# A new order table for a five-engine attention and gated-mixer kernel

## The chip, the cores and the metric

One core of a Trainium2 chip. The time is device microseconds of one execution; of several executions the median is given. The profile is of one execution, taken by the hardware profiler; its span runs from the first to the last instruction.

## What is computed

The reference runs a gated linear recurrence over 768 steps for 4 batches and 8 heads of width 48, and feeds its output, as rows of 384, to a spatially gated mixer:

```python
for t in range(S):
    state = alpha[:, :, t, :, None] * state + einsum('bhd,bhe->bhde', k[:, :, t], v[:, :, t])
    y[:, :, t] = einsum('bhd,bhde->bhe', q[:, :, t], state)
x = y.transpose(0, 2, 1, 3).reshape(B, S, H * D)           # 4, 768, 384
h = maximum(x @ w_in, 0)                                    # 1024 columns
u, v = h[..., :512], h[..., 512:]
v_n = (v - mean(v)) / sqrt(var(v) + 1e-6)                   # over the 512 columns
v_s = einsum('ts,bsd->btd', w_spatial, v_n) + b_spatial[None, :, None]
out = (u * v_s) @ w_out
```

Inputs and output are float32; the matmuls of the kernel take bfloat16.

## The kernel before

**Tiling.** The recurrence is cut into chunks of 128 steps, 6 for each batch, 24 in all, numbered i. The first 8 chunks are done two at a time as pairs 0 to 3 (function `pair`), the rest singly (`first`). For a chunk or pair: ScalarE takes the logarithm of alpha (`lnp`, L446, or `ln`, L654); TensorE sums it along the steps with a triangle of ones (`cump`, L455, or `cum`, L660 and L663); ScalarE takes two exponentials of that (L463 and L472, or L672 and L689); the keys are multiplied by one (`ktp`, L477, or `kt`, L684), the queries by the other (`qtp`, L484, or `qt`); the values are cast (`vbp`, `vb`). TensorE transposes keys and queries (L505, or `trk` L713 for a single chunk); the results are evicted (`ev`). TensorE forms the scores (`sc`, L577 or L748), VectorE masks them (`m`, L588 or L759), TensorE multiplies them by the values (`ya` L604, `y` L617, or `y` L770 and L776). The state's update is a matmul (`updq` L539 and L547, or `upd` L734); `z` adds it (L331, L333), `S` scales it on GpSimd (L338), `sb` casts it. ScalarE casts y (`xs`), TensorE transposes it (`xt`, L368 or L392), `xe` evicts it.

The mixer runs for each batch b: `v`, one group of 3 matmuls a chunk (L822), relu by ScalarE, statistics `bn` (L887, L888), `rs` (L911, L912) and normalization `vn` (L919); `u`, 8 groups of 3 matmuls with relu; `s`, 8 groups of 6 matmuls with w_spatial, emitted in two halves of 3, with the bias added by VectorE (L968) and the gate product `g` (L981) after it; `o`, 6 groups of 4 matmuls, evicted and stored. The last `o` of all is done in two half-width parts (`oh`). w_spatial is transposed on TensorE once (`wt`, L834) and evicted (`we`).

**Kinds of TensorE blocks.** `sc`, `trk`, `wt`, `ya`, `updq` and the `xt` of single chunks use matmuls whose operands hold 48 or 64 rows; the others use all 128 rows.

**What sets the order.** Every operation is an entry of a list; PLAN, a table in the source, names them by number in the order in which they are emitted, with a letter for the engine: P TensorE, D VectorE, A ScalarE, G GpSimd, S a DMA issue on SyncE's queue, Q a DMA as such (which emits nothing). Each engine runs its own operations in the table's order; waits between engines are put in from the data that they share. A P entry can carry numbers, `P43:512:512:192`: matmuls on a tile of constants, so many columns each, put ahead of the block (L188). `replay` (L112) walks the table; `bank` (L176) gives out the 8 PSUM banks in turn. One operation can hold instructions of two engines: operation 3, `("cz", 2)`, is listed under G, and its function `zeros(2)` emits one VectorE memset of `mask4` and three GpSimd instructions (L274, L275, and L279, which fills `mask4` after the memset):

```python
            if n == 2:
                nc.vector.memset(mask4.bitcast(FP32), 0.0)
                nc.gpsimd.memset(ut_ones, 0.0)
                nc.gpsimd.affine_select(
                    out=ut_ones, in_=ut_ones, compare_op=ALU.is_gt, fill=1.0,
                    base=0, channel_multiplier=1, pattern=[[-1, 128]],
                )
                nc.gpsimd.affine_select(
                    out=mask4, in_=mask4, compare_op=ALU.is_gt, fill=1.0,
                    base=0, channel_multiplier=1, pattern=[[0, 4], [-1, 128]],
                )
```

**Loads.** A pair's alpha, keys, queries and values are loaded in 384 KB pieces (L435), those of single chunks in 192 KB pieces (L640) into halves of a tile that two chunks share; weights come in 768 KB pieces (L1072) through two buffers and are cast by any of three engines. Stores are issued at L1037, the two last half-width ones at L1011. All of these go through SyncE's one queue; the bias alone is issued by GpSimd.

Of the kernel before, what the change touches and what calls it, by code (L numbers as in the profile page):

```python
# [62 lines left out]
D176 P138 G185 P83 A139 D175 A80 P140 A84 D186 P178 A143 P180 D179 A177 G187 P188 P190 Q308 S309 D189 G129 P144 P192
D181 A145 D191 A141 G6 D194 A193 A8 P197 D7 Q10 P200 G195 D199 P85 S14 A315 G196 D198 P157 A86 G130 D201 P316 A158
P146 D202 Q312 A317 D159 A318 P203 A147 P204 P208 D87 P88 A205 Q310 A209 G11 P206 D12 P326 A89 D13 P210 A207 D320
P151 S18 Q15 A211 D148 S313 P212 A327 S367 G319 A328 P324 D152 P223 A213 D330 G329 P215 A160 D90 A325 Q19 P334 S371
P322 A216 P221 D162 G16 A224 D217 P153 A222 P332 G17 A91 D323 P229 A335 P225 D92 Q314 S22 D231 A154 P149 D93 A333
G20 D214 P232 A226 P227 A150 Q368 D230 S369 P155 D234 A228 D161 A233 P235 D21 Q372 A218 S409 D237 P238 A236 D219
P344 G321 A156 Q23 D239 P255 S446 D220 G331 P259 D345 A375 P376 D346 P336 A377 A378 A380 P260 D338 Q370 S373 A240
D381 P256 A337 D261 A24 P263 G339 Q410 D257 S411 P264 D25 G379 P241 Q447 D341 P347 A242 S448 D265 P251 A243 G342  # L70
D349 Q374 P244 P383 G340 S413 A245 D246 P252 D348 A417 G262 P275 Q412 A385 S415 D253 P276 D384 G258 A382 Q449 P350
D277 A454 S450 P390 A351 G343 P267 D391 Q414 P418 S480 G278 D392 P354 P352 A419 P279 Q416 A353 S26 G421 P268 A355
P386 A420 A422 P356 D269 Q451 G266 P393 S482 A357 D387 P280 A394 D423 G388 P455 Q481 D281 S484 P395 A457 P425 A456
G389 P361 D427 A424 Q27 D397 G458 A396 S452 P358 D426 A459 A362 D460 P398 G254 A359 D363 P428 A399 P462 G270 P432
D429 A488 P271 D433 A463 G430 Q483 S577 P401 D464 P489 D434 A28 G31 P407 Q485 A490 G30 S486 D400 P272 A492 P435 A402
G491 Q453 D29 P405 S581 A436 D273 P283 G282 A408 D493 Q578 S579 P437 P469 A284 G274 D438 P495 A406 D470 P403 Q487
A496 S611 G461 D471 P287 A439 G431 A497 Q582 D404 P291 S583 A288 D360 P465 P498 Q580 A585 S648 P472 D466 A292 D500
P586 G494 A364 P440 Q612 G467 D499 A587 S690 P295 A473 G468 D366 A588 A590 Q584 S615 P474 A441 G589 P501 D475 D591
P299 Q649 A502 D442 S728 A476 P503 A296 P593 G592 P477 A619 Q691 D505 D504 S613 A300 D594 P517 D365 A478 Q616 P596
D595 S650 P506 A443 D597 A479 D518 P513 Q729 D445 S652 A507 P600 D444 P620 A508 D602 Q614 P519 S692 A621 P533 D509  # L80
A656 P303 Q651 S694 A514 D601 P515 A510 Q653 A622 P525 A698 D512 S617 D511 A624 P529 G623 D516 A520 Q693 P657 S654
P534 A304 D625 G598 A659 A658 P526 D535 Q695 G599 A661 S732 P699 D527 P530 A701 A700 G660 P545 Q618 A703 D531 S730
A736 P627 G536 P603 D629 Q655 P546 S762 A604 D704 G528 P537 A628 D662 Q733 P538 S696 D547 G626 P605 P664 D539 G702
A606 P634 Q731 A607 P630 S766 A665 P541 D631 G663 A666 D635 P737 Q763 G632 P542 S858 A738 D636 G548 A739 P671 A741
P706 Q697 D543 S892 P667 A708 G532 P608 D742 A707 D672 Q767 P521 S764 G740 A609 P637 D633 A770 P549 Q859 A638 S734
D668 P522 D673 P550 Q893 G705 D523 S862 P639 P744 D551 A640 P713 G524 A641 Q765 D746 P674 A745 S860 D714 P771 G669
A675 P642 D715 A772 Q735 G670 S768 A774 P751 P676 A643 P553 G540 D678 Q863 D677 A866 S864 D775 P709 P716 A554 G773
D752 P679 Q861 A717 S929 D753 A900 G544 P557 A680 D710 Q769 D610 S896 P777 G711 A558 P718 P867 A743 G712 Q865 P561
D719 A869 D779 S933 A868 D720 A681 P747 G552 D778 P686 Q930 D644 S894 P721 A871 G870 A562 P754 D748 Q897 A722 D872
S971 P565 G749 A755 D687 G750 A645 Q934 P780 P874 S931 A566 D782 P756 P569 G776 A757 A723 Q895 D781 G873 S975 P573  # L90
D876 A758 A875 P783 D724 Q972 S898 P682 A784 A570 P881 D646 Q932 P785 P759 S973 D787 A786 D883 A574 P788 A937 Q976
D882 S935 A760 P796 D683 A789 P684 Q899 D761 S1012 A797 P877 P800 A685 D790 Q974 A725 P901 S1008 P688 A903 A801 D647
P794 A979 Q936 D726 S1042 P938 A791 D727 P798 D878 A902 Q1013 D792 P810 A940 A905 S1046 D793 G904 P802 A939 D795
P980 Q1009 D906 G879 S1010 P803 A981 P811 G941 A799 D804 Q1043 A942 P806 S977 D689 A982 G805 A984 P807 D812 Q1047
P884 S571 D943 P822 G907 A885 D985 P823 G813 Q1011 D808 S1044 P908 P886 G983 P945 A910 D887 Q978 P814 D909 S1014
A888 D824 P911 A946 G809 P815 D912 Q572 A947 P889 S1048 D816 G944 A1016 Q1045 S575 D880 P987 A890 G817 P915 P952
A988 D916 Q1015 P1017 G913 P830 A1050 D989 A1019 G914 P834 A1018 D917 Q1049 A1021 P1051 D953 G825 P838 A1052 Q576
D954 A835 P948 G1020 P831 A1054 D949 P918 D832 G950 P818 A919 D1022 G986 P819 A839 D1055 G951 P920 P1024 D820 A921
P994 A1025 G1053 D922 P990 P826 D996 A1026 P955 G1023 D995 P827 G833 A956 D991 P1031 D828 P957 P1057 G992 A959 D1032
P923 A958 G821 A1059 D1033 P960 A924 G829 P997 A1058 D925 P967 A998 G993 P1027 A961 P999 P1060 D1028 A968 P842 D962  # L100
G1029 A1000 A1001 P963 G1030 A843 D1061 P1002 A1056 S844 D1062 A964 P1034 S305 A1003 D891 P850 S836 Q845 A1035 S840
P1063 D1004 Q306 P846 A1064 Q837 A926 P1065 P1036 A847 P965 D1067 Q841 D1037 A1038 D1066 P854 D928 D966 P1068 A851
D927 A1005 P969 A1069 D1006 P1074 D1007 P1039 D1070 P1078 A1040 P1080 A855 D1041 P1076 A970 S856 P1090 S297 D1075
A1071 P1094 S285 D1079 A1077 Q857 P1082 S289 D1072 P1106 Q298 D1073 S301 D1081 P1086 Q286 S567 P1087 Q290 S563 P1083
D1088 Q302 S852 P1095 G1089 Q568 P1091 S559 D1096 P1102 Q564 S293 D1092 G1097 P1098 D1084 Q853 S848 P1103 D1093 Q560
G1085 S555 P1099 D1104 Q294 P1107 D1105 P1113 Q849 D1100 Q556 P1117 A1114 D1108 G1101 P1110 D1109 S1115 A1118 P1111
S1119 P1121 D1112 Q1116 P1137 A1122 Q1120 P1125 D1138 S1123 P1133 S1139 A1126 P1129 D1134 Q1124 S1127 S1135 A1130
# [1040 lines left out]
```

## Time and profile before

| | us |
|---|---|
| median of 3 runs | 146.05 (145.07 to 146.84) |
| span of the profiled execution | 142.9 |
| last matmul's end in it | 139.55 |
| last store's landing in it | 141.98 |

The profiled execution's own time outside the span is not recorded; its span is 3.1 us below the median of the runs. In section 1 of the page each engine has its busy time, its share of the span and its instructions; section 2 cuts the span in 40 slices, each digit the busy share in tenths; section 4 is the chain of work that ended last. In lines of the timeline the first number is the start, the second the time to the end of the piece; the piece's own line, operation, output and inputs follow, and in brackets the idle time before it and what ended it. Matmuls are pipelined: a block's cost to TensorE is the distance from its start to the next block's start, not its duration.

### The profile page before, as it was taken

The page shows a single profiled execution, that of the slowest core. Times are in us where ns is not written, and L with a number is a line of the kernel's source. Part 1 is how long each engine was busy: PE and PEld are TensorE (multiplying, and loading weights), DVE is VectorE, ACT ScalarE, POOL GpSimd, SP SyncE. Part 2 cuts the span into 40 slices and gives each one's busy share as a digit, 9 for nine tenths or more (in the row PEclk, how much of TensorE's full clock was granted, in tenths as well). Part 3 has the DMA queues.
Part 4 walks back from the last instruction along what each step waited for, and adds up shares of the span by engine and source line. Part 5 has one row for each costly group of instructions (what it writes and reads, how often), then busy time and mean ns, then how long its engine had stood idle before and what let it go on. Part 6 is the DMA issues. An engine that isn't in the chain of part 4 may idle for free.

```text
span 142.9 us, 4962 instructions
## 1 busy us (share of the span) xinstructions
PE 132.9 (93%) x1910; PEld 83.7 (59%) x1923; DVE 122.2 (85%) x290; ACT 108.2 (76%) x280; POOL 86.0 (60%) x147
## 2 busy tenths in 40 slices
PE   7978977999799999999999999999999999999990
PEld 3464857456465666665655666656666666556460
DVE  6759998998989799989789999889889989776950
ACT  3567398899976799999987889999878688760131
POOL 6945853748317999971288879910999994003700
PEclk9999999999999999999999999999999999999999
DMA  4999989999998999999899999999999103229645
GB/s 115 268 261 265 250 201 327 334 322 328 251 224 163 213 276 161 203 176 198 145 205 192 164 209 162 208 143 206 187 156 222 55 7 137 86 98 338 229 150 180
DMA packets 89000, 28.64 MB, mean 200 GB/s; under 512 B 83728, under 2 KB 87440, under 8 KB 88976
## 3 DMA queue, kind: packets, MB, share of 16 engines
q1 hardware_dynamic: 88944, 28.32, 92.0%
q8 instruction: 15, 0.25, 0.8%
q14 instruction: 9, 0.07, 0.2%
q0 software_dynamic: 32, 0.00, 0.0%
HBM read 23.60 MB, written 4.72 MB: 198 GB/s over the span
## 4 chain that ended last, share of the span: by engine, by line
PE 70%; DMA 10%; SPq 6%; ACT 6%; DVE 3%; issue 2%; ACTq 0%
PE bank L822 50%; DMA ac<-in_alpha_dram 10%; SPq L435 6%; PE bank L748 3%; PE bank L713 3%; PE bank L776 2%; PE bank L660 2%; ACT v_sb L204 2%; PE bank L734 2%; PE bank L770 2%; PE bank L392 2%; DVE stats L887 1%; DVE vn L919 1%; ACT x_sb L198 1%; PE bank L663 1%
## 5 line engine op out<-in xcount | busy, mean ns | idle before, releaser
L822 PE MATMUL bank<-w_spT,vn 128*128 128x384 bf16 x192 | 36.3, 326 | 0.0
L981 POOL TENSOR_TENSOR gT<-vsb,uT 128x384 bf16<-128x384 f32 x28 | 25.8, 928 | 14.2 <-DVE vsb L968 13.5
L822 PEld LDWEIGHTS <-vn 128*128 128x128 bf16 x192 | 16.8, 97 | 10.5 <-DVE vn L919 0.2
L684 POOL TENSOR_TENSOR kt<-kc,binv 128x384 bf16<-128x384 f32 x16 | 14.8, 924 | 12.6 <-ACT bc L679 6.6
L759 DVE TENSOR_TENSOR ptm<-bank,mask 128x512 bf16<-128x512 f32 x32 | 20.8, 683 | 0.6 <-PE bank L748 0.6
L822 PE MATMUL bank<-xT,w_in 128*128 128x384 bf16 x96 | 19.7, 326 | 0.1
L968 DVE TENSOR_TENSOR vsb<-bank,bsp_bc 128x384 f32<-128x384 f32 x31 | 16.6, 552 | 3.0 <-PE bank L822 1.6
L822 PE MATMUL bank<-w_out_sb,gT 128*128 128x384 bf16 (+1 forms) x100 | 18.6, 319 | 0.0
L822 PE MATMUL bank<-w_in,xT 128*128 128x512 bf16 x59 | 16.9, 379 | 1.1 <-issue 0.3
L198 ACT COPY kqT<-bank 128x512 bf16<-128x512 bf16 x26 | 14.8, 592 | 1.3 <-PE bank L713 0.8
L338 POOL TENSOR_TENSOR state<-state,bc 128x192 f32<-128x192 f32 x20 | 10.4, 518 | 8.8 <-ACT bc L553 6.4
L887 DVE BATCH_NORM_STATS2 stats<-v_sb 128x6 f32<-128x512 bf16 x20 | 13.7, 683 | 1.4 <-ACT v_sb L204 1.4
L198 ACT CAST x_sb<-bank 128x384 bf16<-128x384 f32 x24 | 11.5, 485 | 2.2 <-PE bank L776 1.9
L204 ACT ACTIVATE v_sb<-bank 128x512 bf16<-128x512 f32 x20 | 11.6, 601 | 1.6 <-PE bank L822 1.5
L822 PEld LDWEIGHTS <-gT 128*128 128x128 bf16 x100 | 8.9, 97 | 5.6 <-POOL gT L981 0.4
L200 POOL CAST sbd<-state 64x192 bf16<-64x192 f32 x32 | 10.9, 341 | 1.7
L822 PEld LDWEIGHTS <-w_in 128*128 128x128 bf16 x96 | 8.3, 97 | 5.3 <-issue 0.4
L198 ACT COPY xT<-bank 128x192 bf16<-128x192 bf16 (+1 forms) x25 | 8.7, 384 | 2.9 <-PE bank L392 2.6
L919 DVE TENSOR_SCALAR vn<-v_sb,mvs,rstd 128x512 bf16<-128x512 bf16 x24 | 9.8, 437 | 0.7 <-ACT rstd L912 0.7
L588 DVE TENSOR_TENSOR ptm<-bank,mask 128x512 bf16<-128x512 f32 x16 | 10.3, 676 | 0.0
L188 PE MATMUL bank<-junk 128*128 128x512 f32 (+4 forms) x24 | 9.3, 490 | 1.1 <-DVE junk L234 1.1
L200 DVE COPY kqT<-bank 128x512 bf16<-128x512 bf16 x22 | 9.0, 417 | 1.5 <-PE bank L505 0.9
(131 smaller groups left out, 288.2 us busy)
## 6 DMA issues: line engine op xcount, KB each, us to landing
ac<-in_alpha_dram SPq DMA_DIRECT2D x16, 192.0 KB, 4.6
qc<-in_q_dram SPq DMA_DIRECT2D x16, 192.0 KB, 4.7
kc<-in_k_dram SPq DMA_DIRECT2D x16, 192.0 KB, 4.8
vc<-in_v_dram SPq DMA_DIRECT2D x16, 192.0 KB, 4.3
...
```

Of the source, the lines that this page charges most:

```text
L198: nc.scalar.copy(out=out, in_=in_)
L200: ENG[eng].tensor_copy(out=out, in_=in_)
L204: nc.scalar.activation(out=out, in_=in_, func=AF.Relu)
L338: ENG[eng].tensor_tensor(out=st["state"], in0=st["state"], in1=st["bc"][:, :, None].to_broadcast([128, HP, D]), op=ALU.mult)
L588: nc.vector.tensor_tensor(out=st[f"ptm{par}"][:, s], in0=st[f"pt{s}{par}"], in1=mask2[:, par], op=ALU.mult)
L684: ENG[eng].tensor_mul(out=k_blocks(kt3)[:, :, :, 0:D], in0=quad(st["kc"]), in1=st["binv"])
L759: nc.vector.tensor_tensor(out=st["ptm"][:, s], in0=st[f"pt{s}"], in1=mask4, op=ALU.mult)
L822: return lambda ps: nc.tensor.matmul(out=out(ps), lhsT=lhsT(), rhs=rhs(), start=start, stop=stop)
L887: nc.vector.bn_stats(out=stats, in_=d["v_sb"][:, tt, :])
L919: nc.vector.tensor_scalar(out=d["vn"][:, t, :], in0=d["v_sb"][:, t, :], scalar1=d["mvs"][:, t, 0:1], scalar2=d["rstd"][:, t:t + 1], op0=AL ...
L968: nc.vector.tensor_tensor(out=hold["vs"], in0=ps[:, 0:TH], in1=bsp_bc[:, th, :], op=ALU.add)
L981: ENG[eng].tensor_tensor(out=bt[b]["gT"][:, dsl, cols], in0=hold["vs"], in1=bt[b]["uT"][:, dsl, cols], op=ALU.mult)
```

## The change

PLAN is replaced as a whole. It names the same 1141 operations; all 300 TensorE blocks remain. 99 operations are listed under another engine. The matmuls on constants go from 10 blocks with 3040 columns to 8 blocks with 2728. The beginnings, before (-) and after (+):

```diff
-G32 S34 Q33 S36 G0 S38 S40 Q35 D1 Q37 S94 A42 D2 Q39 S96 P43:512:512:192 P53:64 A44 A45 G46 Q41 S98 A54 A55 D47 G56
-D57 P51:512 Q95 P49 S100 P59:64 P61 A58 G48 D60 A50 D52 P63:192 Q97 S163 A62 P247 D65 A102 P71 D248 P74 D72 A64 Q99
-S167 P103:96 G66 P113 D73 A104 A114 D68 D76 A115 Q101 P249 S165 G116 A105 A250 D117 G106 D107 P121:512 Q164 S169 D75
-A122 P111:64 G67 P109 D112 P119 A110 G69 D120 Q168 S4 P131:192 D70 P134 G108 P77 G118 D133 G3 P123:128 A171 Q166
+S34 Q35 S36 Q37 G32 Q33 S38 Q39 G0 S94 Q95 D2 D1 A42 P43:512:512:192 P53 S40 Q41 S96 Q97 A44 A54 D56 G46 P59:424 A55
+A45 D47 D57 P49 P51 P61 P249 S98 Q99 D62 D50 D250 A60 A52 S163 Q164 A102 P74:152 P71 D76 D75 D73 P113 P103 S100 Q101
+A58 G3 G48 P63 A104 A105 A114 A115 A64 D106 D72 D65 G116 S4 Q5 S167 Q168 D117 P109:248 P247 P119 A110 A120 A248
...
```

Numbers of the table that matter here: 3 `cz 2`; 46 and 56 `ktp` of pair 0, 106 and 116 of pair 1; 48 and 58 `vbp` of pair 0; 63 `updq` of pair 0; 65 and 68 `z` of chunks 0 and 1, 66 and 69 their `S`; 71 and 74 `sc` of pair 0, 72, 73, 75 and 76 their `m`; 117 and 107 `qtp` of pair 1; 4 the load of half 1 of w_in.

On SyncE's queue the first loads go from (pair: a alpha, k, q, v) a0 k0 q0 v0 a1 k1 q1 v1 a2 q2 k2 v2 w_in(1) a3 w_in(0) to a0 k0 q0 a1 v0 k1 q1 a2 v1 w_in(1) q2 k2 a3 v2 w_in(0). Five stores instead of one stand ahead of the last input load.

The order on TensorE around the start of the mixer is, before: `wt(2) wt(3) sc(3,0) s(0,1,0) s(0,2,0) cum(8) updq(3)`; after: `wt(1) wt(0) wt(2) sc(3,1) sc(3,0) u(0,3,1) updq(3) s(0,2,0) cum(8)`.

In the loader of single chunks, the first of the two chunks to be loaded now makes the tile that both share, where it was always the even one:

```diff
-                if i % 2 == 0:
-                    T[i + 1][name + "2"] = st[name + "2"] = io_pool.tile([128, 2, H, D], FP32, name=name)
+                if name + "2" not in st:
+                    T[i - i % 2][name + "2"] = T[i + 1 - i % 2][name + "2"] = io_pool.tile([128, 2, H, D], FP32, name=name)
```

The new table has one line less, so line numbers after it are lower by one (L278 for L279).

More of the change, by code (lines that the diff above doesn't have):

```diff
@@ L57 @@
 PLAN = """
-G32 S34 Q33 S36 G0 S38 S40 Q35 D1 Q37 S94 A42 D2 Q39 S96 P43:512:512:192 P53:64 A44 A45 G46 Q41 S98 A54 A55 D47 G56
-D57 P51:512 Q95 P49 S100 P59:64 P61 A58 G48 D60 A50 D52 P63:192 Q97 S163 A62 P247 D65 A102 P71 D248 P74 D72 A64 Q99
-S167 P103:96 G66 P113 D73 A104 A114 D68 D76 A115 Q101 P249 S165 G116 A105 A250 D117 G106 D107 P121:512 Q164 S169 D75
-A122 P111:64 G67 P109 D112 P119 A110 G69 D120 Q168 S4 P131:192 D70 P134 G108 P77 G118 D133 G3 P123:128 A171 Q166
-D132 S307 D125 A124 A78 P172 D136 P81 G126 P182 A173 Q170 S9 D135 P79 A183 D127 A82 P137 A174 Q5 D128 A184 S311 P142
@@ L63 @@
[L63 to L107, printed above, removed]
@@ L108 @@
-Q1140 S1131 Q1128 Q1136 Q1132
+S34 Q35 S36 Q37 G32 Q33 S38 Q39 G0 S94 Q95 D2 D1 A42 P43:512:512:192 P53 S40 Q41 S96 Q97 A44 A54 D56 G46 P59:424 A55
+A45 D47 D57 P49 P51 P61 P249 S98 Q99 D62 D50 D250 A60 A52 S163 Q164 A102 P74:152 P71 D76 D75 D73 P113 P103 S100 Q101
+A58 G3 G48 P63 A104 A105 A114 A115 A64 D106 D72 D65 G116 S4 Q5 S167 Q168 D117 P109:248 P247 P119 A110 A120 A248
+P121:112 D107 G66 P111 S165 Q166 A171 D122 D68 D112 P134:244 D67 P131 P77 D136 D132 D135 G69 G108 G118 G70 P172 A78
+A173 P182 P81 P79 A183 A82 A174 D133 P123 S307 Q308 S169 Q170 G7 P137 A8 A124 A80 D125 D6 G126 P83 P138 G127 S9 Q10
@@ new lines @@
+P85 A184 A139 A84 P142 D186 D128 D176 D185 P140 P88 A86 A141 A143 P190 P180 P144 P188 S311 Q312 A89 A145 S309 Q310
+G175 P178 G177 G129 G130 P157 A189 D191 D87 D181 A179 P200 P197 S14 Q15 A315 A158 A187 P146 P316 P326 D202 D201 D199
+D198 P192 A317 A318 A327 D194 D11 P203:120 G12 P204 A13 A193 A328 A147 D90 S18 Q19 G195 S313 Q314 P149 P153 P155 G196
+S367 Q368 S371 Q372 S369 Q370 D330 D320 A205 A150 P208 P206 P334 A209 A207 P151 P210 P212 P324 D159 D335 D156 D148
+D152 D325 G329 G319 G17 A211 A91 A213 A154 P215 P225 A216 A226 A160 P223 P221 A16 A224 P322 P332 P232 P229 A222 A233
@@ new lines @@
+A323 A234 G20 D214 D92 D93 D333 D217 D231 D230 D162 P235:212 D161 D236 P347 S22 Q23 P344 P227 G21 G321 S409 Q410 A237
+A331 P336 D349 D348 D345 D338 S411 Q412 S373 Q374 S446 Q447 S413 Q414 S450 Q451 A218 A375 D219 D220 P259 P376 P263
+P251 A378 A337 A377 A380 A228 D346 P260 P252 P255 D381 D261 D253 G339 G379 D341 G25 G340 G342 P264 P256 D265 A24 P238
+D257 P383 A239 P241 D240 A384 P244 D385 P350 G254 G382 D245 D242 D243 A417 P390 P354 S448 Q449 A246 P418 D343 D392
+D391 A351 A419 A355 A420 A422 P267 P279 P352 P268 P280 P356 D269 A353 P358 P386 D387 S480 Q481 A454 A357 P455 P275
@@ new lines @@
+A359 D423 D281 G421 G258 G388 G389 S415 Q416 A456 P393 S482 Q483 A394 A457 A459 P276 P425 S484 Q485 G262 G458 G266
+D277 P395 P361 A396 A397 D426 D460 A427 S452 Q453 P403 D360 P432 A488 A362 P462 S26 Q27 G424 P489 P407 P401 S577 Q578
+D433 D434 A464 A404 A490 G491 A492 D463 P428 D429 D408 A402 P271 P435 P272 D493 A436 P469 D273 P437 P495 S486 Q487
+S581 Q582 S579 Q580 G430 P398 G431 G274 G282 D471 D470 P405 A461 A438 A496 A439 A399 P472 D497 D363 P440 A473 A28 A31
+D30 P498 P474 P465 D475 D406 A441 A585 G29 A364 A476 G270 G278 G494 D500 D499 D466 G467 D366 D442 D400 P291 P283 A292
@@ new lines @@
+P586 P477 P299 G468 P295 A588 A587 A284 G589 A478 A590 A300 D591 D365 P501 P303 A296 A502 A443 P593 A594 P503 P287
+S583 Q584 S613 Q614 G592 S611 Q612 S648 Q649 S652 Q653 S617 Q618 S615 Q616 S650 Q651 D505 D504 A304 A479 P506 P596
+P517 D595 D444 D445 P600 A507 A508 A288 A619 A656 A518 D597 D602 D601 D509 A510 P515 P513 P533 P519 P620 D520 P525
+A621 A514 P657 A659 A626 A622 P529 A658 A624 S690 Q691 S654 Q655 S728 Q729 D512 D511 P526 D516 G598 G623 G660 P534
+P537 D527 D625 D535 A661 P530 P630 D631 D531 P538 P627 P545 S694 Q695 S692 Q693 S732 Q733 P603 A698 A628 A604 D662
@@ new lines @@
+D629 D539 P546 G536 G532 G632 G663 D547 G548 G599 S730 Q731 P664 P605 P634 A736 D665 D666 A606 A607 P541 P737 A738
+P699 P667 A701 A739 D636 D635 P542 A700 A703 P521 P608 P522 S762 Q763 S696 Q697 S858 Q859 A741 D668 D543 D704 G702
+G633 G740 G528 A609 D742 P671 P706 D523 D673 D672 G524 P549 A707 A708 P637 P550 A638 A770 D551 P713 P639 P744 D715
+D745 D714 A641 P674 P557 S766 Q767 S734 Q735 S764 Q765 S862 Q863 A640 A746 P642 A866 A675 A558 D610 P751 P676 P771
+D677 A643 A705 A772 D678 D752 D753 G669 G670 G552 G544 G540 P553 P867 P561 P709 A774 A869 A868 A562 A554 A871 D644
@@ new lines @@
+D775 D710 G773 G743 G711 P716 A717 P565 P679 G712 D872 P777 P718 A566 A680 A645 A779 P747 P684 D720 D719 D748 D778
+D685 S929 Q930 S860 Q861 G870 G749 P754 P721 A755 A681 P780 P756 P874 A757 A722 S768 Q769 G776 G750 S971 Q972 S933
+Q934 S892 Q893 S864 Q865 G873 S896 Q897 S898 Q899 S894 Q895 S973 Q974 P682 P688 P686 A875 A723 A876 D758 D782 D781
+D683 D646 D689 P783 P759 A784 P881 P785 D724 D687 A760 P569 P573 S975 Q976 S931 Q932 D787 D761 D883 D882 A786 A937
+P794 P788 P798 A725 A570 A900 A979 A789 A574 A795 D647 D727 D790 D726 D799 P796 P877 P800 P901 P980 P938 P810 P806
@@ new lines @@
+A907 A791 D792 D793 A902 A797 A903 A981 A905 P811 D878 A982 A801 A939 A940 A942 P814 P807 D812 D906 A984 G983 G904
+G879 G941 P815 P884 P822 A885 D808 D943 D985 D816 P802 P823 D824 P886 P908 P945 A888 A887 P803 D909 D946 D804 P911
+P889 S301 Q302 S935 Q936 S1042 Q1043 A1050 D947 A944 A910 A890 D912 P987 P915 D988 P952 S1046 Q1047 S1008 Q1009 A989
+A1016 S1010 Q1011 S567 Q568 S977 Q978 S1012 Q1013 S1014 Q1015 D916 D953 D917 D954 G880 G813 G809 G913 G817 G805 P818
+P830 P1051 P948 P1017 A1052 A1019 A1018 A1054 G825 P819 G1020 G986 G914 D820 P838 P831 D1055 D949 D832 P918 P834 A839
@@ new lines @@
+A1021 D1022 A919 P994 P920 A921 A835 P1024 P826 G950 S297 Q298 S1044 Q1045 S575 Q576 S293 Q294 S1048 Q1049 S836 Q837
+S571 Q572 S563 Q564 S840 Q841 S555 Q556 G821 G1053 D995 P990 P955 A1025 A1023 A956 P827 P842 D996 D922 D1026 D991 G992
+D828 G951 P957 P1031 P1057 A958 A843 D959 P1027 P969 P963 P997 D1032 D1033 D1028 D1059 D1058 P923 A970 A998 A964 G833
+G993 G1056 G1029 G1030 G829 P1060 P999 D1000 D1061 D1062 A1001 P1034 P960 P1002 P1063 A1035 A924 D925 D891 A1064 A961
+A1003 P850 P1036 P1065 A926 A851 P854 D1066 D1037 D1067 D1038 P846 P1068 D1004 D962 D927 P967 P1076 P1074 P1039 A1069
@@ new lines @@
+A1005 A855 A847 A1040 A968 P965 P1078 P1080 D1006 D928 D1007 D1070 S559 Q560 S285 Q286 S856 Q857 S289 Q290 S852 Q853
+S848 Q849 S305 Q306 S844 Q845 D1041 D1077 D1081 A1075 A1071 A966 D1072 D1073 D1079 P1090 P1094 P1098 P1082 P1086 P1083
+P1110 P1087 P1095 P1102 P1091 P1099 P1111 P1106 D1084 D1088 D1085 D1096 D1092 G1089 G1097 P1103 D1100 D1093 D1112
+G1101 P1107 D1104 P1117 D1108 G1105 P1113 D1109 A1118 S1119 Q1120 P1137 A1114 P1133 D1138 S1115 Q1116 P1121 A1134
+S1139 Q1140 S1135 Q1136 P1125 A1122 P1129 S1123 Q1124 A1126 S1127 Q1128 A1130 S1131 Q1132
```

## The prediction

> **What bounds the kernel now.** I read the page's busy times and slices first, then busy time by stretch, then the chain of work around the point where it changes engine, then single TensorE blocks in the timeline.
>
> ```profile
> span 142.9 us, 4962 instructions
> PE 132.9 (93%) x1910; PEld 83.7 (59%) x1923; DVE 122.2 (85%) x290; ACT 108.2 (76%) x280; POOL 86.0 (60%) x147
> PEclk9999999999999999999999999999999999999999
> DMA  4999989999998999999899999999999103229645
> PE 70%; DMA 10%; SPq 6%; ACT 6%; DVE 3%; issue 2%; ACTq 0%
> ```
>
> The clock is full throughout, so nothing is to be gained there. DMA is full until about 110 us. The chain is 70% TensorE. By stretch (columns: TensorE, its weight loads, VectorE, ScalarE, GpSimd):
>
> ```profile
> 30.00:35.00 5.00, 5.00 (x54) 3.09 (x51) 4.45 (x12) 4.94 (x14) 3.43 (x4) 1.00 1.03 343
> 35.00:40.00 5.00, 4.24 (x80) 2.37 (x73) 4.96 (x16) 4.83 (x14) 1.78 (x3) 1.00 1.16 271
> 40.00:45.00 5.00, 5.00 (x104) 3.19 (x103) 4.52 (x10) 3.08 (x8) 1.77 (x3) 1.00 0.90 173
> 45.00:50.00 5.00, 5.00 (x101) 3.25 (x94) 4.10 (x8) 4.01 (x10) 4.62 (x9) 1.00 1.20 206
> ```
>
> From 30 to 40 us VectorE and ScalarE are full and TensorE still waits; from 40 us TensorE is full. The chain changes hands here:
>
> ```profile
> 37.95 0.32 DVE vn L919
> 38.28 0.48 DVE w_row L200
> 38.76 0.05 issue
> 38.80 0.35 PE bank L834 x12
> 39.15 0.35 PE bank L577 x16
> 39.50 1.08 PE bank L822 x6
> ```
>
> From 38.80 to the last matmul's end at 139.55 us TensorE waits for hardly anything (its blocks' excess over their usual spacing adds to under 1 us). So two quantities set the time: when the mixer of batch 0 gets going, and how much TensorE work is left then, gaps included. After the last matmul come an eviction (0.48) and a store (landed 141.98).
>
> **What the order costs TensorE by itself.** Blocks whose matmuls use half of the rows (transposes of keys and queries, scores, L834 weight transposes, the pair's state update and outputs) do not follow full-row blocks for free:
>
> ```profile
> 53.75 0.36 PE L734 MATMUL bank<-vb,kt 128*128 128x48 bf16 x8
> 54.05 0.29 PE L713 MATMUL bank<-ident,kt 64*128 64x64 bf16 x8
> 54.17 0.28 PE L713 MATMUL bank<-ident,qt 64*128 64x64 bf16 x8
> 54.29 0.39 PE L748 MATMUL bank<-kqT 48*128 48x128 bf16 x8
> 54.61 0.66 PE L822 MATMUL bank<-w_spT,vn 128*128 128x384 bf16 x3
> ```
>
> Read the starts. The transposes (54.05 to 54.29) cost 0.24 before another half-row block; the scores cost 0.32 (54.29 to 54.61) before a full one. Elsewhere in this trace scores before a half-row block cost 0.23 to 0.25, transposes before a full one 0.34, the update L734 0.20 before a full block and 0.29 or 0.30 before a half-row one, three-matmul mixer blocks 0.49 and 0.58. So going in and coming out of half-row blocks costs 0.09 to 0.10 each, 0.19 per excursion. [...]
>
> **The change part by part.**
>
> 1. *Order on TensorE.* All 300 blocks remain. Block s(0,2,0), first half, is number 70 in both orders; it starts at 39.93 before. Of the 69 blocks ahead, two differ: before has one mixer half (0.49) and one weight transpose (0.28) there, after has the update of pair 3 (0.78) and a score (0.25): 0.26 us more done. From block 70 on, I count 25 excursions to half-row blocks before and 21 after: 4 x 0.19 = 0.76. Work left after block 70 falls by 0.76 + 0.26 = 1.0 us.
>
> 2. *When block 70 starts.* Laid out by hand with the rows' durations; the after order gives the sequence on each engine.
>  - Loads: the 384 KB loads land about 1.5 us apart (4.34, 5.85, 7.37, 8.88, ... 14.94). Alpha of pair 1 moves to slot 4 (8.88 instead of 10.39), alpha of pair 2 to slot 8 (14.94 instead of 17.82); half 1 of w_in passes q, k and v of pair 2, whose landings go from 19.24, 20.60, 22.62 to about 21.2, 22.4, 24.7.
>  - GpSimd takes its step "cz 2" before the value cast of pair 0 instead of after pair 1. That step holds an L279 select which waits for a VectorE memset:
>
> ```profile
> 17.42 0.29 POOL L275 TENSOR_SCALAR_AFFINE_SELECT ut_ones<-ut_ones 128x128 bf16<-128x128 bf16 x1
> 18.24 0.63 POOL L279 TENSOR_SCALAR_AFFINE_SELECT mask<-mask 128x512 bf16<-128x512 bf16 x1 [0.53 <-DVE mask L273]
> ```
>
>    After, that memset stands behind three maskings of scores on VectorE. Scores come at about 9.8 to 10.4, three maskings of 0.6 end at 12.3, memset 12.5, select 13.2, value cast (0.50) 13.75. Behind the cast on GpSimd wait the key product of chunk 1 and the two state scalings. The update of pair 0 on TensorE can start at 13.8; without the wait it would be about 11.2 (values land 10.39, ScalarE's cast of the other half ends 10.96). It was at 9.61 before. State z(0), in VectorE's queue ahead of pair 1's query products, then ends at 15.0, query products at 15.95 (14.53 before), scores of pair 1 at 17.15 (15.91 before), y block of pair 0 at 17.75 (16.49). VectorE did the maskings meanwhile, so it has less idle time, and the maskings of pair 1 end at 20.45 against 20.17.
>  - ScalarE: logs of pair 2 at 16.9 (17.85 before), but it then waits for pair 0's y; x cast 18.35 (18.65), fourth exponential of pair 2 at 21.65 (21.02), since the w_in cast and an x eviction go ahead of it. VectorE waits for this about 0.9 us. Pair 2's last masking ends at 28.6 (28.05).
>  - From there both queues are full. ScalarE needs 28.0 us of back-to-back work up to the variance step rs(0,4), where before needs 25.8: it gains 13 operations (6.4 us: two weight casts 0.61 and 0.84, six evictions of 0.48, two value casts, two w_spT evictions, a bias) and loses 9 (4.2 us). With its waits squeezed, pair 3's value cast ends at 39.2 and the update of pair 3 starts at 39.25 (40.68 before, but two blocks later in the order). VectorE's last vn of batch 0 comes at about 41.2 (39.92), just before TensorE wants it at 41.8. Block 70 starts at 40.05.
>
>    Bounds: 38.7 if the memset wait costs nothing that lasts (13.8 minus the 11.2 to 12.4 at which keys would allow it, some 1.3 us); 41.9 if ScalarE keeps all the idle time it had before at rs(0,4) (worked out under the rivals). I take 40.05, +0.1 us, nearest to the layout.
>
> 3. *Waits after block 70.* The chains get shorter: from transposes to the scores of the same chunk at least 1.0, 1.4 and 1.4 us of TensorE work (before at least 1.6); v to the mixer in batch 2 3.5 (3.9 the shortest before). One ScalarE eviction takes 0.59 and the way through v (0.60), statistics (0.87), rs (0.50) and vn (0.44) 2.4 plus the gaps, so most fits if the queue ahead is empty. Lower bound 0; upper 2 us (about 1 us less lead of VectorE's queue over TensorE's order in six stretches, on two batches). I take 0.5.
>
> 4. *Engine moves.* 99 operations change engine; by mean rows VectorE gains 0.3 us, ScalarE loses 0.7, GpSimd 1.6. Off the path after 40 us (ScalarE 3.08 of 5.00 busy at 40 to 45); before it they are in step 2.
>
> 5. *Loads and stores in the late half.* More stores stand between the last input loads (five ahead of the last value load, one before). At some 0.6 us of queue each, keys of chunk 23 slip to about 112 us and queries of chunk 22 from 102.5 to about 110; TensorE wants both chunks' transposes about 2 to 2.6 us later, against a product of 0.92 or 0.55. Zero, on that cover; if it is gone, up to 1 us. SP queues stores behind outputs long finished, zero.
>
> 6. *Tail.* Last block, last eviction and last store are as before. The final pair of mixer groups now ends 1.3 us of TensorE work ahead of the block that needs them. The last gate product runs on VectorE beside one on GpSimd: such a pair took 0.91 (135.45) where it takes 0.55 alone (132.74). Evictions 0.56, then 0.91, then TensorE about 0.25 late; before it lost 0.34 near its last group. Zero. [...]
>
> 7. *Fills* (matmuls on junk, 3040 to 2728 columns) stand in waits: zero, but the 212 before a weight transpose at 37 us (0.4) are in step 2. The edit in the loader only chooses who makes a pair's buffer: no instruction, zero.
>
> Sum: -1.0 + 0.1 + 0.5 = -0.4. Span 142.9 to 142.5; the median of the runs (146.05) lies 3.1 above the profiled span, so 145.7.
>
> **The rivals.**
> - *The start gains* (ends faster): alpha lands 1.5 and 2.9 us earlier and the memset wait is absorbed. Block 70 at 38.7: 145.7 - 1.35 = 144.3. For: VectorE has its maskings done while GpSimd waits. Against: z(0) stands ahead of the query products.
> - *ScalarE is the bound of the start* (ends slower): its 2.2 us more work before rs(0,4) is not squeezed out of its idle time. Before, rs(0,4) ended at 38.73 after 25.8 us of work, 12.9 idle. If that stays, the value cast ends at 27.6 + 0.4 + 12.9 = 40.9, the update of pair 3 (0.78) and the way back to full rows (0.1) follow, and block 70 starts at about 41.9: 145.7 + 1.85 = 147.5. It decides (over 1% slower) from 12.9 us of idle kept upwards; at 11.2 it is the layout above. For: ScalarE 4.94 and 4.83 of 5.00 busy already.
> - *Late waits* (3 above at its upper end, with 5 uncovered): +2.5: 148.2. For: 1.0 us between transposes and scores. Against: TensorE lost under 1 us in the same way before.
> - *The change doesn't do what its placing is for*: the 0.76 of excursions is not gained, for the blocks then wait for their inputs instead: 146.5, inside the forecast's range.
>
> **How the numbers follow.** A measurement of this kernel tells about 1% from no change (runs of before 145.07 to 146.84). Forecast with its fourth rival, 144.7 to 147.4: 0.47; start gains, 143.6 to 144.6: 0.20; ScalarE 0.22 and late waits 0.11, both from 147.5 up. So faster 0.20, same 0.47, slower 0.33. Range 144.0 to 148.2: half of the gain case's spread below and the late waits' price above; about 2 in 10 lie outside.
>
> **What would show it.** Step 1: from block 70 to the last matmul under 99.6 us; scores and transposes in longer runs. Step 2: a GpSimd wait of over 3 us for the DVE memset at L278, the cast behind it near 13.2, TensorE's update of pair 0 near 13.8; block 70 near 40. Step 3: new TensorE waits under VectorE or ScalarE evictions after 45 us. Wrong if the first stretch, which I laid out by hand, is off by more than 1.3 us, or if a queue is blocked by a wait that I priced at nothing.

## The result, and the profile after

The changed kernel takes 151.47 us (median of 4 runs, 150.35 to 153.09), the kernel before beside it 145.99 (145.07 to 146.84): a ratio of 1.035, 95% interval 1.026 to 1.044. The ratio leaves out the run of 153.09 us, which lies over 1.5% above the fastest. Forecast were 145.7 and a range of 144.0 to 148.2. The profiled execution is that longest one, so its trace shows more lost than a typical run has; how much more is told under e4.

The page of the changed kernel, the lines that answer to those shown of before:

```profile
span 151.3 us, 4957 instructions
PE 138.5 (92%) x1919; PEld 87.0 (57%) x1919; DVE 120.5 (80%) x292; ACT 108.0 (71%) x279; POOL 84.9 (56%) x146
PEclk9997558999999999599999999999999999999999
PE 71%; ACT 7%; issue 6%; POOL 6%; DVE 4%; DMA 3%; POOLq 0%; DVEq 0%; ACTq 0%
```

The third line is what has changed: the granted clock of TensorE, all nines before, has a dip in slices 4 to 7 and one in slice 17. TensorE is busy 5.6 us longer than before with the same blocks, because some of them ran at a granted clock of 0.50. By stretch (columns as before: length, TensorE, its weight loads, VectorE, ScalarE, GpSimd, granted clock, DMA share, GB/s):

```profile
10.00:15.00 5.00, 2.48 (x73) 1.97 (x75) 4.07 (x9) 2.99 (x6) 1.86 (x3) 0.83 1.27 261
15.00:20.00 5.00, 5.00 (x38) 3.44 (x31) 2.47 (x7) 2.47 (x5) 1.25 (x3) 0.50 1.16 314
20.00:25.00 5.00, 5.00 (x152) 4.01 (x152) 3.56 (x8) 2.69 (x8) 2.31 (x6) 0.65 0.98 227
...
55.00:60.00 5.00, 2.37 (x53) 1.45 (x52) 1.88 (x4) 2.56 (x8) 3.44 (x5) 1.00 0.93 245
60.00:65.00 5.00, 5.00 (x74) 3.02 (x66) 3.52 (x10) 3.09 (x8) 2.06 (x4) 0.66 1.04 190
```

Read each group downwards. TensorE stands still for half of a stretch (busy 2.48 of 5.00 us from 10 to 15, 2.37 from 55 to 60), and in the next stretch it is full at a lower clock (0.50 and 0.66). In the start all other engines are less busy then: VectorE 2.47, ScalarE 2.47 and GpSimd 1.25 of 5.00. They wait for TensorE now, not it for them.

Where each stop comes from, in the timeline (start, duration, engine, line, what, and in brackets the idle time before it and what ended it). The first, on GpSimd and TensorE:

```profile
13.14 0.83 POOL L278 TENSOR_SCALAR_AFFINE_SELECT mask<-mask 128x512 bf16<-128x512 bf16 x1 [4.64 <-DVE mask L272]
13.93 0.49 POOL L199 CAST vbp<-vc 128x384 bf16<-128x384 f32 x1
...
11.62 0.34 PE L538 MATMUL bank<-halves_of,la 128*128 128x2 bf16 x8
14.47 0.82 PE L546 MATMUL bank<-vbp,kt 64*128 64x48 bf16 x32 [2.52 <-POOL vbp L199]
...
43.76 0.66 PE L821 MATMUL bank<-w_spT,vn 128*128 128x384 bf16 x3
```

The kernel before has the same 32 matmuls here:

```profile
9.89 0.57 PE L547 MATMUL bank<-vbp,kt 64*128 64x48 bf16 x32
```

The select waits 4.64 us for VectorE's memset, the value cast stands behind it, and these matmuls of updq(0) start at 14.47. This chain was forecast, 0.7 us earlier. The last line of the changed kernel's is block 70: 43.76, against 39.93 before and 40.05 forecast. The second stop, on VectorE, GpSimd and TensorE:

```profile
54.36 0.55 DVE L967 TENSOR_TENSOR vsb<-bank,bsp_bc 128x384 f32<-128x384 f32 x1
58.12 0.56 DVE L967 TENSOR_TENSOR vsb<-bank,bsp_bc 128x384 f32<-128x384 f32 x1 [3.20 <-POOL gT L980]
...
56.30 0.91 POOL L683 TENSOR_TENSOR kt<-kc,binv 128x384 bf16<-128x384 f32 x1
57.17 0.91 POOL L980 TENSOR_TENSOR gT<-vsb,uT 128x384 bf16<-128x384 f32 x1
...
59.52 0.40 PE L747 MATMUL bank<-kqT 48*128 48x128 bf16 x8 [2.63 <-DVE qt L693]
```

The eviction of s(0,2,1) waits for the product g(0,3,0), although it doesn't use its result. It wants the buffer that this g reads: `vs_bufs` has four tiles, given out in turn (L985 and L965), and this eviction can only go when the g of the one four back, listed ahead of it, has read. GpSimd had kt(10) ahead of that g. Behind the eviction on VectorE stand the transposed keys' copy and qt, and TensorE's scores sc(9) wait for these.

TensorE's last matmul ends at 147.90; from block 70 to it are 104.14 us (99.62 before). So of the 8.35 us by which this execution's matmuls end later than those of before, 3.83 arise ahead of block 70 and 4.52 after it.

### The profile page after: what moved, and what is told of

It reads as the page before. It is cut to its first block, busy times and chain, and to the rows that moved or that the text cites. A ratio compares the mean times of both kernels' runs of the same rounds, so it can differ in the third digit from the quotient of the medians.

```text
span 151.3 us, 4957 instructions
## 1 busy us (share of the span) xinstructions
PE 138.5 (92%) x1919; PEld 87.0 (57%) x1919; DVE 120.5 (80%) x292; ACT 108.0 (71%) x279; POOL 84.9 (56%) x146
## 4 chain that ended last, share of the span: by engine, by line
PE 71%; ACT 7%; issue 6%; POOL 6%; DVE 4%; DMA 3%; POOLq 0%; DVEq 0%; ACTq 0%
PE bank L821 45%; POOL gT L980 3%; PE bank L747 3%; DMA ac<-in_alpha_dram 3%; PE bank L712 2%; DVE vsb L967 2%; PE bank L775 2%; PE bank L187 2%; PE bank L454 2%; PE bank L733 2%; PE bank L769 2%; PE bank L659 2%; PE bank L546 2%; PE bank L576 2%; ACT xT L197 1%
## 5 line engine op out<-in xcount | busy, mean ns | idle before, releaser
L821 PE MATMUL bank<-w_spT,vn 128*128 128x384 bf16 x192 | 36.9, 332 | 0.0
L758 DVE TENSOR_TENSOR ptm<-bank,mask 128x512 bf16<-128x512 f32 x32 | 20.4, 680 | 0.8 <-PE bank L747 0.8
L821 PE MATMUL bank<-w_in,xT 128*128 128x512 bf16 x72 | 19.3, 380 | 0.4 <-ACT xT L197 0.2
L821 PE MATMUL bank<-xT,w_in 128*128 128x384 bf16 x96 | 18.8, 328 | 0.0
L197 ACT COPY kqT<-bank 128x512 bf16<-128x512 bf16 x22 | 12.7, 591 | 6.6 <-PE bank L712 4.3
L199 POOL CAST sbd<-state 64x192 bf16<-64x192 f32 x36 | 12.3, 341 | 1.9
L199 DVE COPY kqT<-bank 128x512 bf16<-128x512 bf16 x26 | 10.4, 414 | 3.0 <-PE bank L504 2.9
L187 PE MATMUL bank<-junk 128*128 128x512 f32 (+8 forms) x20 | 10.0, 612 | 1.1 <-DVE junk L233 1.1
L197 ACT COPY o_sb<-bank 128x384 f32<-128x384 f32 x9 | 4.2, 476 | 9.3 <-PE bank L821 9.3
L587 DVE TENSOR_TENSOR ptm<-bank,mask 128x512 bf16<-128x512 f32 x16 | 10.1, 681 | 0.7 <-PE bank L576 0.6
```

The lines of the kernel that those rows point to most:

```text
L187: nc.tensor.matmul(out=flat[:, 0:cols].rearrange("p (a b) -> p a b", a=4), lhsT=junk, rhs=junk[:, None, 0:n].to_broadcast([128, 4, n]), st ...
L197: nc.scalar.copy(out=out, in_=in_)
L199: ENG[eng].tensor_copy(out=out, in_=in_)
L587: nc.vector.tensor_tensor(out=st[f"ptm{par}"][:, s], in0=st[f"pt{s}{par}"], in1=mask2[:, par], op=ALU.mult)
L758: nc.vector.tensor_tensor(out=st["ptm"][:, s], in0=st[f"pt{s}"], in1=mask4, op=ALU.mult)
L821: return lambda ps: nc.tensor.matmul(out=out(ps), lhsT=lhsT(), rhs=rhs(), start=start, stop=stop)
```

## The experiments

Theory T has two causes, both a stop of TensorE of some 2.5 us and a clock that is halved after it (0.50 and 0.66 in the stretches above): one in the start (mask4's memset), one at 57 us (the buffers that go round in turn, the ring). In the table, block 70 is the start of s(0,2,0), "rest" runs from there to the last matmul's end, both in the profiled execution. A "half window" is as much half clock as the changed kernel's second dip has (0.50 from 61.06 to 64.48 us): 3.41 us, a third of its first dip (0.50 from 13.28 to 23.52, 10.24 us). Their number is an estimate for each run, rounded, from its mean clock and span: (1 - clock) x 2 x span / 3.41 us. For the changed kernel's profiled run (0.955, 151.3 us) that gives 4.0.

| kernel | block 70 | rest | half windows by run | ratio to before |
|---|---|---|---|---|
| before | 39.93 | 99.62 | 0 in the profiled | 1 |
| changed | 43.76 | 104.14 | 4, 2, 2, 3 | 1.035 (1.026 to 1.044) |
| e1 mask early | 39.55 | 102.90 | 0, 1, 0, 1 | 1.0245 (1.019 to 1.030) |
| e2 fill in the wait | 40.88 | 104.08 | 1, 1, 1, 1 | 1.036 (1.032 to 1.041) |
| e3 eight buffers | 41.25 | 100.10 | 1, 2, 1, 1 | 1.012 (1.006 to 1.018) |
| e4 both e1 and e3 | 40.08 | 100.40 | 0 in 10 runs | 0.9999 (0.997 to 1.003) |
| e5 g ahead of kt | 39.91 | 102.06 | 0, 0, 0, 1 | 1.016 (1.009 to 1.023) |
| e6 six buffers | 39.72 | 101.90 | 0, 0, 0, 1 | 1.013 (1.007 to 1.019) |
| e9 e3 with e2's fills | 40.80 | 99.81 | 0 in 12 runs | 1.0043 (1.002 to 1.007) |

Block 70 and rest are of single executions. e1, e4, e5 and e6 have the same order in the start, and their block 70 lies between 39.55 and 40.08, so about 0.5 us there can be chance. The profiled executions of before and e4 differ by 1.0 us in span (142.9 and 143.9), while the medians of their runs are equal (145.21 and 145.20).

**e1: the memset one group earlier.**

```diff
             if n == 1:
                 ...
                 nc.vector.memset(eps_tile, LN_EPS)
+                nc.vector.memset(mask4.bitcast(FP32), 0.0)
             if n == 2:
-                nc.vector.memset(mask4.bitcast(FP32), 0.0)
                 nc.gpsimd.memset(ut_ones, 0.0)
```

> The changed kernel with one line moved: VectorE's zeroing of mask4 goes from the last group of zeros (cz 2) to the one before it, so that GpSimd's select on mask4 finds it done and the value cast behind that select no longer waits. Theory T (the late value cast lets TensorE idle 2.5 us, after which its granted clock is halved for some 10 us): block s(0,2,0) starts at 39.8 to 40.5 instead of 43.76, no half clock before 45 us, the whole run 2 to 3.7 us shorter: 147 to 149 us, ratio to the kernel before 1.01 to 1.02. Rival R1 (ScalarE and VectorE are the bound of the start, the clock only follows them): the wait moves to another operand, block s(0,2,0) still at 43 or later, time 150 to 151.5. Rival R2 (the wait itself costs, the clock does not matter): 0.7 us less, the length by which the cast missed its forecast.

148.60 us, as T has it, but a ratio of 1.0245, above T's 1.02; block 70 at 39.55, below what any theory said; the clock is whole in the profiled run (mean 1.0). R1 falls: with the wait gone, nothing else takes its place in the start. R2 had 0.7 us: 4.2 came back at block 70 against the changed kernel's longest run, 2.9 in the medians. The stop at 52 us is still there, alone, and two of the four runs lost a window. e1's waits of TensorE:

```profile
PE bank L747 <- DVE qt L693: 2.6, 1, 2.6
```

**e2: the wait kept, TensorE kept busy.**

```diff
-A58 G3 G48 P63 A104 A105 ...
+A58 G3 G48 P63:512:512:192 A104 A105 ...
```

> The changed kernel with the wait left as it is and work that serves nothing put into it: three fills (matrix products on a constant tile, 512, 512 and 192 columns) ahead of updq(0), the block that waits for the value cast. T: TensorE's clock stays whole through the wait, the wait remains, so block s(0,2,0) starts at 40.5 to 41.3 and the run is 2 to 3 us shorter than the changed kernel: 147.5 to 149.5 us. R1 and R2 (the clock does not matter): no gain, 150.5 to 152 us, or worse by the length of the fills that outlasts the wait.

Block 70 at 40.88, as T has it, but the time is 150.28 us, above T's band: no gain on the changed kernel that can be told. The profile of e2, two stretches and two lines of TensorE:

```profile
15.00:20.00 5.00, 4.58 (x106) 3.52 (x104) 4.30 (x11) 3.40 (x7) 2.93 (x7) 1.00 1.16 315
...
55.00:60.00 5.00, 3.36 (x38) 2.19 (x39) 3.64 (x8) 1.75 (x4) 1.46 (x3) 0.66 1.15 261
...
11.25 2.21 PE L187 MATMUL bank<-junk 128*128 128x512 f32 x6
14.11 0.57 PE L546 MATMUL bank<-vbp,kt 64*128 64x48 bf16 x32 [0.47 <-POOL vbp L199]
```

The fills stand in the wait, and updq(0), at 14.11 almost as late as in the changed kernel, takes 0.57 and not 0.82. The first dip is gone (1.00 where the changed kernel has 0.50). Each of the four runs has one half window (mean clock 0.988 or 0.989), in the profiled one at the second stop, and if that stop took one from each run of the changed kernel too, that kernel's two runs at 150.35 and 150.39 us had lost one in the start, not the three of the profiled one. So the expectation, read off the longest run, was too large. What one window in the start is worth had to be measured without the second stop: e3 and e9.

**e3: eight s buffers.**

```diff
-                hold["vs"] = vs_bufs[turn[1] % 4]
+                hold["vs"] = vs_bufs[turn[1] % 8]
...
-    vs_bufs = [small.tile([128, TH], FP32, name=f"vsb{n}", bufs=1) for n in range(4)]
+    vs_bufs = [small.tile([128, TH], FP32, name=f"vsb{n}", bufs=1) for n in range(8)]
...
-        d["uT"] = batch.tile([128, NDS, S], BF16, name="uT")
+        d["uT"] = batch.tile([128, NDS, S], BF16, name="uT", bufs=2)
```

> The changed kernel with eight s buffers in place of four (paid for by two u tiles in place of three, which the order's own sequence leaves room for). With four buffers in the new order the evictions of s(0,0,1), s(1,2,1), s(1,3,1) and s(2,0,0) take a buffer whose old content its g has yet to read, so four gates are computed from another block's s; with eight each g reads its own. T: s(0,2,1)'s eviction no longer waits 3.2 us for GpSimd, TensorE's 2.6 us stop at 57 us and the half clock after it go; the start stays as it is; 2.7 to 4.4 us shorter: 146.8 to 149 us. Rival R3 (GpSimd is simply behind with its g, the ring only passes that on): the wait comes back a few us later at another g or o, gain under 1.5 us, 149.5 to 151 us.

146.53 us, 0.3 below T's band. R3 falls: the wait doesn't come back elsewhere, and a wait of 0.97 us for another g, at 117 us in the changed kernel, went too. The start keeps its wait, but this time the clock fell for one half window (0.66 from 15 to 20 us, 1.00 from 20 to 25) and not three (0.50 from 13.28 to 23.52 in the changed kernel): block 70 at 41.25. TensorE's line at the end of the wait, still at full clock (1.00 from 10 to 15 us):

```profile
14.07 0.58 PE L546 MATMUL bank<-vbp,kt 64*128 64x48 bf16 x32 [2.51 <-POOL vbp L199]
```

The four gates that the expectation names bear on more than time: with four buffers (the changed kernel, e1, e2, e5) they hold a wrong factor. The output moves little by it: in the reference's inputs s is 1 (b_spatial) plus sums over 768 products with numbers of some 0.01/768, which is about 0.0004 by estimate.

**e4: both.** The edits of e1 and e3.

> The changed kernel with both repairs, mask4 zeroed early and eight s buffers. T: the two losses add up, nothing else of size is left after them: clock whole from 6 us to the end, block s(0,2,0) at 40 us, last matrix product at 139.5 to 141, time 145 to 146.7 us, ratio to the kernel before 0.993 to 1.006, which is what the prediction had for the changed kernel. Rival R4 (the new order is worse in many small places): 147.5 us or more.

145.20 us beside 145.21 of before: as T has it, and R4 falls. e4's page, stretches and TensorE:

```profile
span 143.9 us, 4942 instructions
PEclk9999999999999999999999999999999999999999
...
10.00:15.00 5.00, 4.48 (x98) 3.10 (x97) 4.86 (x11) 3.92 (x10) 1.92 (x3) 1.00 1.28 264
15.00:20.00 5.00, 4.41 (x157) 3.52 (x156) 4.38 (x11) 3.21 (x9) 2.15 (x5) 1.00 1.15 310
...
11.62 0.57 PE L546 MATMUL bank<-vbp,kt 64*128 64x48 bf16 x32
40.08 0.66 PE L821 MATMUL bank<-w_spT,vn 128*128 128x384 bf16 x3
```

updq(0) is the same 32 matmuls that took 0.82 after the stop and take 0.57 here. The two losses of the changed kernel's profiled run are 43.76 - 40.08 = 3.68 and 104.14 - 100.40 = 3.74; their sum, 7.42, is the difference of the spans, 151.3 - 143.9 = 7.4. In a typical run the first is smaller. By the ratios, e3, which keeps the first stop, takes 1.2% more than before, and e1, which keeps the second, 2.5% more; together 3.7%, beside 3.5% of the changed kernel. So the ring costs about twice what the memset does, and the profiled execution shows the memset's share too large.

**e5 and e6: the second stop in doses.** e5 is e1 with two entries swapped, e6 is e4 with six buffers:

```diff
-... G262 G458 G266
+... G262 G266 G458
...
-    vs_bufs = [small.tile([128, TH], FP32, name=f"vsb{n}", bufs=1) for n in range(8)]
+    vs_bufs = [small.tile([128, TH], FP32, name=f"vsb{n}", bufs=1) for n in range(6)]
```

> e1_mask_early (mask4 zeroed early, four s buffers) with two entries of the order swapped: on GpSimd g(0,3,0), for which s(0,2,1)'s eviction waits, goes ahead of kt(10), which took 0.91 us in front of it. T (TensorE's stop at 52 us is the eviction's wait, and the clock falls only after a long stop): the stop goes from 2.69 to 1.8 us, the half clock that two of e1's four runs had is not seen or seen in one at most, time 146.5 to 147.6 us, ratio 1.010 to 1.016. Rival R5 (kt(10), now 0.9 us later, is what sc(9) and sc(10) wait for next): the stop stays near 2.5 us, 148 to 149 us.

> e4_both with six s buffers in place of eight: s(0,2,1)'s eviction then waits for g(0,2,0), which ends 1.7 us ahead of g(0,3,0). T: a stop of 0.8 to 1.1 us near 52 us, no half clock in any run, time 145.8 to 146.5 us, ratio 1.003 to 1.009; with four, six and eight buffers the time falls by the length of the stop. R3 (GpSimd is behind anyway): no difference to e4, 145.2 us.

147.10 and 146.65 us. e5 is as T expected, its ratio at the upper end; R5 and R3 fall. The stop at 52 us is 2.6 us in e1, 1.8 in e5, 0.9 in e6 and absent in e4, by what is taken out ahead of the one g. e5's row, then e6's:

```profile
PE bank L747 <- DVE qt L693: 1.8, 1, 1.8
```

```profile
PE bank L747 <- DVE qt L693: 0.9, 1, 0.9
PE bank L747 <- DVE vsb L967: 0.8, 1, 0.8
PE bank L391 <- DVE ptm L758: 0.8, 1, 0.8
```

But e6's time missed its band (ratio 1.013 for 1.009 at most): the second and third row are new, at 83 to 85 us, where a later eviction now meets a g still queued. With six buffers in the ring the place of the wait moves; with eight there is none.

**e7 and e8: what the fills do.** All numbers behind P entries are taken out, of the kernel before (e7) and of e4 (e8):

```diff
-... P43:512:512:192 P53:64 ...
+... P43 P53 ...
```

> The kernel before with all its ten fills taken out (3040 columns of matrix products that serve nothing, all ahead of 20 us). T (a TensorE that is not kept busy loses its clock): half clock in two to five windows of the first 25 us, block s(0,2,0) at 41.5 to 44 instead of 39.93, time 147 to 150 us. Rival R6 (the prediction's step 7: fills stand in waits and are worth nothing either way; the start is paced by loads and the other engines): 145 to 145.8 us, or shorter, if TensorE's waits soak up the lost clock.

> e4_both without its eight fills (2728 columns; those of ya(2) and wt(2) at 28 and 36 us among them). T: as e7, two to five half windows, block s(0,2,0) at 41.7 to 44.5, time 147 to 150 us. R6: 145 to 145.8 us. If only one of e7 and e8 loses, it is the length of the waits left in its start that decides, 1.6 us at most in e4 and 1.04 in the kernel before.

e7: 147.76 us, ratio 1.019 (1.016 to 1.022), block 70 at 42.05. e8: 146.31, ratio 1.009 (1.006 to 1.011), block 70 at 41.82. R6 falls in both, e8 loses less than T gave it. The stretches show nothing of it: they print a clock of 1.00 from 0 to 40 us in both. The matmuls show it. e7, TensorE's timeline:

```profile
11.41 1.07 PE L577 MATMUL bank<-kqT 48*64 48x128 bf16 x32
...
18.77 0.82 PE L604 MATMUL bank<-vbp,ptm 64*128 64x48 bf16 x32
...
22.36 0.58 PE L604 MATMUL bank<-vbp,ptm 64*128 64x48 bf16 x32 [0.24 <-DVE ptm L588]
```

and the kernel before:

```profile
10.65 0.64 PE L577 MATMUL bank<-kqT 48*64 48x128 bf16 x32
...
16.49 0.57 PE L604 MATMUL bank<-vbp,ptm 64*128 64x48 bf16 x32
```

The same scores take 1.07 instead of 0.64, and the same output block goes from 0.82 to 0.58 within e7. In the changed kernel the same two blocks take 1.07 and 0.82 at a granted clock of 0.50 (at 20.02 and 21.02 us), so the start of e7 is read here as run at half clock. Its matmuls are slow from 8.21 us on at the latest (0.61 for four transposes that take 0.40 in before) until after 20.88 (0.53 for a sum that takes 0.33); at 21.47 two sums take 0.49, as in before, where at 13.02 they took 0.85. Half speed over these 12.7 us would be 6.3 us lost, and at block 70 2.1 us are lost (1.7 in e8): by this estimate much of it is soaked up by waits for loads and for the other engines, not all.

**e9: the wait without the half clock, and without the second stop.** e3 with e2's fills.

> e3_ring8 with the three fills of e2 ahead of updq(0): no stop at 57 us that could lower the clock a second time, mask4 zeroed late as in the changed kernel, so that the 2.5 us wait stays and only the clock is held. T (wait and clock are two costs): no half clock in any run, block s(0,2,0) at 40.7 to 41.0, time 145.6 to 146.3 us, ratio 1.003 to 1.008, between e4 (neither wait nor half clock, 145.2) and e3 (both, 146.5). If the clock is worth nothing here: as e3, ratio 1.012. If the wait is worth nothing and only the clock counts: as e4, ratio 1.000.

145.96 us, block 70 at 40.80, as T expected. Against e4 the wait alone costs 0.72 us at block 70 (0.4% of the time), little more than single executions differ by. Against e9, three half windows cost 2.96 us at block 70 in the changed kernel's profiled run (43.76). One costs 0.45 in e3 (41.25), which could be chance, and the intervals of e3 and e9 overlap slightly too (1.006 to 1.018, 1.002 to 1.007); so the price of one window in the start is not settled. At the second stop the window costs 1.2 us: the rest is 102.90 in e1 without and 104.08 in e2 with it.

**e10 to e12: two waits of the start filled.** e4 has two waits left in its start. e10 moves xe(0) ahead of a weight cast and u(0,3,1) into TensorE's wait before wt(2); e11 adds the means of v(1,4) and v(1,5) earlier. Both leave u(0,3,1)'s eviction so late that its PSUM bank is overwritten first, so their output is wrong. e12 is e10 with that eviction moved along:

```diff
-... P137 A8 A124 A80 ...
+... P137 A80 A8 A124 ...
-... P235:212 D161 D236 P347 S22 Q23 P344 P227 G21 G321 S409 Q410 A237 ... A228
+... P227 P235 D161 D236 P347 S22 Q23 P344 G21 G321 S409 Q410 A228 A237 ...
```

> e4_both with two moves in the order of the start: on ScalarE the eviction xe(0), for which v(0,0) waited 0.80 us, ahead of a cast of the weights; on TensorE u(0,3,1) ahead of wt(2), which waited 0.66 us after a fill for a cast on GpSimd, and that fill taken out. T7 (each wait is local, and other work that is ready fills it): 0.45 and 0.7 us come off, time 144.0 to 144.6 us, ratio 0.991 to 0.996. Rival R7 (ScalarE, busy 4.99 of 5 us from 20 to 25 us, is the bound there): what is taken off comes back at a later eviction, 145.0 to 145.4 us, ratio 0.998 to 1.002.

> e10_start_order and, at 68 to 73 us, the means of v(1,4) and v(1,5) (mv on VectorE, then rs on ScalarE) and their vn ahead of m(12), ln(14), u(1,2,1) and u(1,3,1), since block s(1,3,0) waited 0.5 us for vn. T7: 0.3 to 0.5 us off e10, 143.6 to 144.2 us, ratio 0.988 to 0.993. R7: as e10, or later by what m(12) and ln(14) lose, 0.3 us.

> e10_start_order with u(0,3,1)'s eviction A228 placed ahead of A237. In e10 (and e11) it stood so late in the order that the PSUM bank, of which there are eight in rotation, was handed on before the eviction had read it; those two kernels' u(0,3,1) is therefore not u, and only their times are to be read. Here each block's bank is read first. T7: the time of e10, 144.2 to 144.9 us, ratio 0.991 to 0.996. Rival R7: the eviction, now in front of those of wt(2), ln(8) and cum(8) on ScalarE, delays them and block s(0,2,0), 145.0 to 145.6 us, ratio 0.998 to 1.002.

e10: 144.58 us, ratio 0.993 (0.991 to 0.995), block 70 at 39.41. e11: 144.40, 0.994 (0.991 to 0.997): the vn edit gains nothing. e12: 144.66, 0.996 (0.993 to 0.999), block 70 at 39.60. So, with its two stops out and two waits filled with work that was ready, the new order takes some 0.4% less than the old (e12, the only one of the three with the right output; its interval leaves 0.1 to 0.7%). R7 as put (ratio 0.998 at least) falls with e10's interval; e12's reaches just into it. About half of the 1.15 us hoped for came: 0.67 us at block 70 in e10 and 0.48 in e12. In e10 the wait before v(0,0) went from 0.80 to 0.24 and that before wt(2) from 0.66 to nothing, and a wait of 0.46 came up behind wt(2)'s first matmul.

## Why the prediction was wrong

Two steps failed. Step 2 had no price for the clock, and step 3 no wait for the four s buffers; in a typical run the second cost more.

**Step 2, When block 70 starts (+0.1 expected, +3.8 in the profiled run, +1.3 in e3).** The chain was right: the select, the cast behind it, updq(0) late. It came at 14.47 for 13.8. What failed is how it was costed: the layout by hand took every TensorE block at its duration of before, under the sentence "The clock is full throughout, so nothing is to be gained there". Nothing was to be gained, but something to be lost. From 13.28 to 23.52 us the blocks ran at half clock (0.50), and the clock's fall is caused by the wait that the step itself had found (e2 and e9 keep the wait, hold the clock, and have block 70 at 40.8 to 40.9). The bounds, 38.7 to 41.9, were drawn from queues alone, so they hold e3's 41.25, with one half window, and not 43.76, with three. The wait's own price is 0.72 us (e9 against e4); the step's lower bound, which takes it away, had it at 1.35.

**Step 3, Waits after block 70 (+0.5 expected, 0 to 2), the larger loss in a typical run.** What failed is the list of what an operation waits for. It was made of data, and the four s buffers are no data: the table's check on order (`replay`) doesn't know them either. The distance between an eviction and the g four back falls to one entry in the new table (g(0,3,0) directly ahead of s(0,2,1)), and in four places an eviction is even listed ahead of the g whose buffer it takes. In the old table the shortest such distance is 11 entries. Price: 2.5 us in e1 against e4, with a half window 3.7. The last line of the prediction named the case, "a queue is blocked by a wait that I priced at nothing", but no term held it. The chains that the step did go through, transposes to scores and v to the mixer, hold: in e4 the longest wait of TensorE after 42 us is 0.36 us, for a vn.

**Step 7, Fills: "stand in waits: zero".** Wrong as a rule: without them both kernels lose 1.7 to 2.1 us at block 70 (e7, e8). For this change the term was about right, since the new table keeps most of its fills in the first 20 us; it has none in the one wait that it adds.

**Step 1, Order on TensorE (-1.0).** Neither shown nor refuted. The step's sign, a rest under 99.6 us, didn't come: e4, without the two stops, has 100.40, e9 99.81 and before 99.62, where steps 1 and 3 together gave 99.1. Whether the excursions bring less or more small waits came up can't be told from these, since single executions differ by as much. So the fourth rival, that the 0.76 of excursions is not gained, stays open.

**Steps 4 to 6.** Step 4's moves hardly show: VectorE, ScalarE and GpSimd are busy 122.2, 108.2 and 85.2 us in e4, 122.2, 108.2 and 86.0 in before. No stop of TensorE after 42 us ends at a load, so step 5's zero stands. At the tail the last gate product took 0.88 us beside GpSimd's, for 0.91 in step 6, and TensorE stood 0.16 us for it.

**The rivals.** "ScalarE is the bound of the start" fell with e1: with the memset early, ScalarE's queue as in the changed kernel, block 70 starts at 39.55. "Late waits" had the side and, for the ring's stop alone, the size (+2.5), by luck: its waits were those of chains within a chunk. "The start gains" would have needed 38.7. The sum itself, 145.7, is close to what the new order takes without its two stops, 145.2 in e4, but that is luck too: e4 has no memset wait, for which step 2 gave 38.7 and 40.08 was measured, and its rest is 1.3 us above steps 1 and 3. No term of the sum had the half clock.
